# Three edits at the start of a fused state-attention and gated-projection kernel: a shorter first group of unread products, a constant first step on ACT, and the order of two loads

## The chip, the cores and the metric

The kernel runs on one core of a Trainium2 chip. The metric is device time in microseconds (us). The engines are TensorE (PE, with its weight loads shown as PEld), VectorE (DVE), ScalarE (ACT), GpSimd (POOL) and SyncE (SP), which issues the DMAs.

## What is computed

The reference has two stages. Cut to what matters:

```python
scores = (x @ state.T) / sqrt(D)                  # x: 8 x 8 x 512 x 64, state: 8 x 8 x 32 x 64
xread  = softmax(scores)  @ state                 # tokens read the state
sread  = softmax(scores.T) @ x                    # the state reads the tokens
x2     = concat([xread, sread], tokens)           # 8 x 576 x 512
gate   = sigmoid(sum(conv_w[k] * shift(x2, k)))   # causal convolution, 5 taps
out    = (gate * (x2 @ w_val)) @ w_out
```

All data is float32.

## The kernel before

The program is a list of numbered steps. `op(fn, ...)` appends one; the string `ORDER` says in which order they are issued, with a letter for the engine where a step may run on several (`a` ACT, `v` DVE, `g` POOL). Each engine works through its own instructions in that order, with semaphores between engines. So a number that moves in `ORDER` moves all that its step issues, on each engine it uses. Another table, `SLOTS`, gives every tile its buffer.

The eight batches follow each other, overlapped: scores on PE (`scores`, L386), maxima and 32x32 transposes on DVE (`max_n`, `probs`, L459, L469, L391), exponentials on ACT (L476, L396), subtraction of the maximum and the scaling on POOL (the helper at L238), reads of the state (L513 for batch 0, L498 for the others), values (L562), gates, and the output projection in three float32r terms (L571 to L573). Batch 0 is split in two runs of 256 tokens. The first run's data comes with the state in `first_in` (L263), the second run's in `rest_in` (L273), and both runs write the same two banks of PSUM, `sc`: DVE's transposes of the first run come before PE's second.

The convolution's taps come as 64-bit words, loaded by `load_conv` (L285, tile `cww`, 20 KB). ACT takes two parts of them (`words_part` L312, `words_side` L320, tiles `wt` and `ws`), DVE joins them (L328, L337, tile `cv`), and PE spreads them over partitions (L294, `cwbp`) for batch 0's reads. The weights `w_val` and `w_out` (tiles `vw` and `ow`) are joined in the same way; POOL does some of the parts (L322, `ws_v`).

`warm_up` (L347) issues products of a constant tile `blank` with itself, which nobody reads; `WARM` gives how many products each of four groups has. Step 955 is the first group and stands ahead of the first scores, 956 and 957 come after the second run, 958 ahead of the transposes `e2p` (L403). A product is two matmul records.

The steps at the start that the change and the prediction speak of: 66 `load_first`, 67 `load_xT` of batch 0 (`rest`), 6 `load_conv`, 69 and 70 `scores` of the two runs, 955 to 958 the unread products. Constants are set ahead of all steps: `blank` by DVE, `ident`, `edge`, `ex`, `sum2` and `own` by POOL. `own` (128x4) is a mask, 0 but for 1 in one column per group of 32 partitions; it is read only by `last_tokens`, far later.

A DMA uses one of eight semaphore lanes in turn, and a DMA that comes to a lane again waits for the landing of the one before it there.

Of the kernel before, what the change touches and what calls it, by code (L numbers as in the profile page):

```python
# [13 lines left out]
AF = mybir.ActivationFunctionType  # L14
# [24 lines left out]


STATES = 4
WARM = (8, 2, 5, 6)
TAP_COUNT = 5
ENGINES = dict(a="ACT", v="DVE", g="POOL")
ORDER = """
13 66 955 67 69 6 18 72 23 7 71 70 73 87 8a 89 9 74g 80 956 79 75 155 10 19 0 81 957 16 90 14 20g 76 82g 11 958 21 17a
77g 25a 38 24 15a 22 83 4 88 106g 53 94 92 1 26 84 157 85g 33 91 35g 27 95a 93a 28 100 78 12a 39 86 102a 158 101a 107
40a 30g 166 55a 54 262 167 41 168 56 159 57 160 29 42 169 34 111 113 115 112 116 31 2 119 264 36 32 37 114 120 117a
161g 273 265 43 58a 118g 59g 162 103 45a 68 44 104a 105a 121a 46 180 163 143 131 48 122g 64a 47 274 164g 137 123 149
# [69 lines left out]
def state_attention_gated_kernel(  # L119
# [17 lines left out]
    nc = tc.nc  # L137
    B, _, NJ, H, D = x_in.shape
    S, NPR, NS = NJ * P, sT_in.shape[3], sT_in.shape[4]
# [69 lines left out]
    def op(fn, *args):  # L209
        steps.append((fn, args))  # L210

    for name, shape, dt in (
# [6 lines left out]
    ident, wv, woh, wol, cv, cwt, edge, z, xt, ex, sum2, own, blank = (  # L219
        fixed[n,] for n in ("ident", "wv", "woh", "wol", "cv", "cwt", "edge", "z", "xt", "ex", "sum2", "own", "blank"))  # L220
# [441 lines left out]
    nc.gpsimd.memset(edge, -EDGE)  # L662
    nc.gpsimd.memset(ex[..., NS:], EPS)
    nc.gpsimd.memset(sum2, EPS)
    nc.gpsimd.memset(own, 0.0)
    for q in range(NPR):
        nc.gpsimd.memset(own[NS * q:NS * q + NS, q:q + 1], 1.0)

# [97 lines left out]
    def tail():  # L766
        for k in range(NPR):
            op(high, lambda k=k: weight_parts("wvh")[:, k], lambda k=k: wv[:, k])
            op(low, lambda k=k: weight_parts("wvl")[:, k], lambda k=k: wv[:, k], lambda k=k: weight_parts("wvh")[:, k])
        op(tail_high)  # L770
        op(tail_low)
        for m in range(2):
            for c in range(2):
                op(tail_first, m, c)
            for c in range(2):
                op(tail_taps, m, c)
            op(tail_gate, m)
            for c in range(2):
                op(tail_values, m, c)
            op(tail_gated, m)  # L780
            op(high, lambda m=m: get("tgh", m), lambda m=m: get("tg", m))
            op(low, lambda m=m: get("tgl", m), lambda m=m: get("tg", m), lambda m=m: get("tgh", m))
        for r in range(NR):
            for k in range(NPR):
                op(tail_project, r, k)
            op(tail_copy, r)
            op(tail_store, r)
# [25 lines left out]
    tail()  # L813
    for i, n in enumerate(WARM):
        op(warm_up, i, n)
# [55 lines left out]
```

## Time and profile before

| | |
|---|---|
| three runs | 205.43, 205.28, 204.87 us; median 205.28 |
| profiled execution | 205.45 us, of which the span of the trace is 203.6 |
| mean granted TensorE clock | 0.989 |
| PE busy | 194.9 us, 96% of the span |
| DVE busy | 171.4 us, 84% |
| POOL busy | 153.3 us, 75% |
| ACT busy | 144.4 us, 71% |
| DMA | 39.69 MB, 194 GB/s of HBM traffic over the span |

The profiled execution is 1.85 us longer than its span, the time from the first to the last instruction. Busy shares are means over the whole run; the stage that the change touches is the first 17 us of it.

### The profile page before, as it was taken

The numbers are of one execution on the slowest core, as the hardware profiler recorded it, in microseconds if no ns is written. First come the engines' busy times: TensorE is split into PE (matmuls) and PEld (weight loads), VectorE is DVE, ScalarE is ACT, GpSimd is POOL, SyncE is SP. The second block draws the span as 40 slices with busy tenths as digits, with TensorE's granted clock in tenths as the row PEclk, the third lists the DMA queues.
The fourth block names the chain that finished last, engine by engine and source line by source line (L and its number), as shares of the span: only waits on it lengthen the run. The fifth ranks groups of instructions, "written<-read, shape, count | busy, mean of one in ns | idle before, by whom it ended". The sixth has DMA issues, their size and how long they took to land.

```text
span 203.6 us, 4484 instructions
## 1 busy us (share of the span) xinstructions
PE 194.9 (96%) x1709; PEld 143.4 (70%) x1709; DVE 171.4 (84%) x278; ACT 144.4 (71%) x296; POOL 153.3 (75%) x119
## 2 busy tenths in 40 slices
PE   7599989799999999999999999999999999999993
PEld 7495344478567866687588557886876788899882
DVE  1898896999998999999999999999997995867002
ACT  0789996676988499878876989569947996612031
POOL 2594778797994889579997999599988998882200
PEclk9969999999999999999999999999999999999999
DMA  6999796059207928962982516250980380001736
GB/s 231 366 380 358 262 401 240 5 200 380 93 0 267 390 30 276 354 235 91 282 349 112 200 25 241 106 194 32 321 282 3 154 293 18 0 3 39 272 87 222
DMA packets 14787, 39.69 MB, mean 195 GB/s; under 512 B 1434, under 2 KB 5934, under 8 KB 12846
## 3 DMA queue, kind: packets, MB, share of 16 engines
q1 hardware_dynamic: 14766, 39.41, 54.3%
q8 instruction: 13, 0.21, 0.4%
q14 instruction: 8, 0.07, 0.1%
HBM read 26.30 MB, written 13.11 MB: 194 GB/s over the span
## 4 chain that ended last, share of the span: by engine, by line
PE 85%; DVE 9%; ACT 2%; issue 2%; DVEq 0%
PE val L562 22%; PE op L571 13%; PE op L572 13%; PE op L573 13%; PE xr L498 3%; PE warm L347 3%; PE tval L639 3%; PE sc L386 3%; PE xr L513 2%; PE sgv L357 2%; PE srp L427 2%; DVE g L567 2%; DVE sl L459 1%; DVE nb L391 1%; DVE acc L542 1%
## 5 line engine op out<-in xcount | busy, mean ns | idle before, releaser
L542 DVE SCALAR_TENSOR_TENSOR acc<-xr,cwt,acc 128x510 f32<-128x510 f32 (+2 forms) x84 | 59.1, 732 | 1.3 <-ACT xt L538 0.6
L571 PE MATMUL op<-woh,gh 128*128 128x512 f32 x124 | 50.3, 406 | 0.0
L572 PE MATMUL op<-wol,gh 128*128 128x512 f32 x124 | 48.4, 390 | 0.0
L573 PE MATMUL op<-woh,gl 128*128 128x512 f32 x124 | 48.3, 390 | 0.0
L238 POOL TENSOR_TENSOR gl<-g,gh 128x512 fp32r<-128x512 f32 x32 | 41.1, 1295 | 6.1 <-ACT gh L225 5.8
L238 POOL TENSOR_TENSOR acc<-acc,last 128x508 f32<-128x508 f32 x28 | 35.8, 1286 | 11.2 <-DVE acc L542 7.5
L571 PEld LDWEIGHTS op<-woh,gh 128*128 128x128 f32 x124 | 23.3, 188 | 11.6 <-issue 3.5
L573 PEld LDWEIGHTS op<-woh,gl 128*128 128x128 f32 x124 | 23.3, 188 | 5.0
L572 PEld LDWEIGHTS op<-wol,gh 128*128 128x128 f32 x124 | 23.3, 188 | 4.7 <-issue 0.5
L567 DVE SCALAR_TENSOR_TENSOR g<-sig,val 128x512 f32<-128x512 f32 x32 | 21.4, 675 | 5.0 <-PE val L562 2.1
L233 ACT ACTIVATE last<-xr,cwt 128x508 f32<-128x508 f32 x28 | 19.3, 698 | 5.3 <-DVE acc L542 3.7
L554 ACT ACTIVATE sig<-acc 128x512 f32<-128x512 f32 x28 | 17.9, 640 | 5.2 <-POOL acc L238 5.1
L225 ACT CAST gh<-g 128x512 fp32r<-128x512 f32 x29 | 18.1, 634 | 4.8 <-DVE g L567 4.8
L537 ACT ACTIVATE acc<-xr,cwt 128x512 f32<-128x512 f32 x28 | 19.2, 703 | 2.8 <-PE xr L498 2.8
L238 POOL TENSOR_TENSOR sl<-sl,mx 128x1024 f32<-128x1024 f32 (+1 forms) x9 | 15.6, 1729 | 6.9 <-DVE mx L469 6.9
L225 ACT COPY o<-op 128x512 f32<-128x512 f32 (+1 forms) x26 | 14.4, 570 | 7.0 <-PE op L573 5.1
L238 POOL TENSOR_TENSOR al<-sl,ah 128x1024 fp32r<-128x1024 f32 x7 | 16.8, 2397 | 1.1 <-ACT ah L225 1.1
L238 POOL TENSOR_TENSOR ex<-ex,rc 128x1024 f32<-128x1024 f32 (+1 forms) x9 | 15.5, 1723 | 2.5 <-DVE rc L481 2.3
L562 PE MATMUL val<-ah,swh 128*128 128x512 f32 x56 | 16.8, 396 | 0.5 <-DVE acc L542 0.3
L562 PE MATMUL val<-al,swh 128*128 128x512 f32 x56 | 16.8, 390 | 0.0
L562 PE MATMUL val<-ah,swl 128*128 128x512 f32 x56 | 16.4, 389 | 0.0
L227 DVE COPY o<-op 128x512 f32<-128x512 f32 x7 | 4.8, 690 | 13.7 <-PE op L573 13.7
(122 smaller groups left out, 375.4 us busy)
## 6 DMA issues: line engine op xcount, KB each, us to landing
x<-x_in SPq DMA_DIRECT2D x8, 1024.0 KB, 6.0
out<-o SPq DMA_DIRECT2D x31, 256.0 KB, 3.0
xT<-xT_in SPq DMA_DIRECT2D x7, 1024.0 KB, 6.6
turned<-eb SPq DMA_DIRECT2D x7, 512.0 KB, 3.0
e2T<-turned SPq DMA_DIRECT2D x7, 512.0 KB, 5.5
vw<-w_val SPq DMA_DIRECT2D x4, 511.8 KB, 6.8
ow<-w_out SPq DMA_DIRECT2D x4, 511.8 KB, 8.4
xT<-first_in SPq DMA_DIRECT2D x1, 576.0 KB, 3.4
```

The costliest lines, as they stand in the source:

```text
L225: nc.scalar.copy(out, in_)
L233: nc.scalar.mul(out, in_, factor)
L238: (nc.vector if e == "DVE" else nc.gpsimd).tensor_tensor(out, a, b, op=how)
L347: nc.tensor.matmul(get("warm", i)[:, j % 4 * P:j % 4 * P + P], blank, blank, start=True, stop=True)
L537: nc.scalar.mul(get("acc", b, pr), pt, cw[:, HALO, pr:pr + 1])
L542: nc.vector.scalar_tensor_tensor(acc[:, d:], get("xr", b, pr)[:, :S - d], cw[:, HALO - d, pr:pr + 1], acc[:, d:], op0=ALU.mult, op1=ALU.add)
L554: nc.scalar.activation(get("sig", b, pr), get("acc", b, pr), AF.Tanh, scale=0.5)
L562: nc.tensor.matmul(get("val", b, k), w[:, g, c], a[:, g], start=(term == 0 and g == 0), stop=(term == terms - 1 and g == NG - 1))
L567: nc.vector.scalar_tensor_tensor(get("g", b, k), get("sig", b, k), 1.0, get("val", b, k), op0=ALU.add, op1=ALU.mult)
L571: nc.tensor.matmul(pt, gh, woh[:, k], start=(k == 0), stop=False)
L572: nc.tensor.matmul(pt, gh, wol[:, k], start=False, stop=False)
L573: nc.tensor.matmul(pt, gl, woh[:, k], start=False, stop=(k == NPR - 1))
```

## The change

The first group of unread products has seven products and not eight. The load of the taps is issued ahead of the load of `rest`. The mask `own` is zeroed by an ACT instruction on the constant `blank`, relu(-1 x 1), in place of POOL's fill; it is ACT's first instruction, and the table load that precedes ACT's first activation comes with it. The rest of the order is kept.

```diff
-WARM = (8, 2, 5, 6)
+WARM = (7, 2, 5, 6)
...
 ORDER = """
-13 66 955 67 69 6 18 72 23 7 71 70 73 87 8a 89 9 74g 80 956 79 75 155 10 19 0 81 957 16 90 14 20g 76 82g 11 958 21 17a
+13 66 955 6 69 67 18 72 23 7 71 70 73 87 8a 89 9 74g 80 956 79 75 155 10 19 0 81 957 16 90 14 20g 76 82g 11 958 21 17a
...
-    nc.gpsimd.memset(own, 0.0)
+    nc.scalar.activation(own, blank[:, :NPR], AF.Relu, scale=-1.0)
     for q in range(NPR):
         nc.gpsimd.memset(own[NS * q:NS * q + NS, q:q + 1], 1.0)
```

SP's queue at the start of the program, before (left of the arrow is the tile written; `DMAHW1` is lane 1, and a wait on it here is for the landing of the DMA that had lane 1 last):

```order
L263 DMA xT_97<-first_in 128x1152
L273 DMA rest<-rest_in 128x1152
L285 DMA cww<-conv_w 20x511
L281 DMA vw_0_122<-w_val 128x2047
L269 DMA z<-z_in 128x512 [waits DMAHW0_49]
L281 DMA ow_3_212<-w_out 128x2047 [waits DMAHW1_49]
L281 DMA vw_3_239<-w_val 128x2047 [waits DMAHW2_49]
```

and now:

```order
L263 DMA xT_97<-first_in 128x1152
L285 DMA cww<-conv_w 20x511
L273 DMA rest<-rest_in 128x1152
L281 DMA vw_0_121<-w_val 128x2047
L269 DMA z<-z_in 128x512 [waits DMAHW0_49]
L281 DMA ow_3_211<-w_out 128x2047 [waits DMAHW1_49]
L281 DMA vw_3_238<-w_val 128x2047 [waits DMAHW2_49]
```

The taps and `rest` have changed places and lanes: lane 1 is now that of the taps, for which the `ow` behind `z` waits, and lane 2 that of `rest`.

ACT's queue from its first instruction on, before:

```order
L312 ACT_TABLE_LOAD [waits DMAHW2_49]
L312 ACTIVATE wt_conv<-cww,edge 20x128 [waits Pool_49]
L320 ACTIVATE ws_conv<-cww,edge 20x128
L476 ACTIVATE ex<-sl_124 128x2x8x32 [waits Pool_49]
L312 ACTIVATE wt_v_159<-vw_0_122,edge 128x512 [waits DMAHW3_49]
```

and now:

```order
L665 ACT_TABLE_LOAD
L665 ACTIVATE own<-blank 128x4 [waits DVE_49]
L312 ACTIVATE wt_conv<-cww,edge 20x128 [waits DMAHW1_49,Pool_49]
L320 ACTIVATE ws_conv<-cww,edge 20x128
L476 ACTIVATE ex<-sl_123 128x2x8x32 [waits Pool_49]
L312 ACTIVATE wt_v_158<-vw_0_121,edge 128x512 [waits DMAHW3_49]
```

The table load no longer waits for a DMA, and one activation stands behind it; the wait for the taps is now that of the first tap step.

POOL's queue behind its fills of `ex` and `sum`, as a difference:

```order
-L665 MEMSET own 128x4
 masks.py:199 ISA
 masks.py:199 AFFINE_SELECT ident<-ident 128x128 [waits Pool_49]
-L667 MEMSET own 32x1 [waits Pool_49] x2
+L667 MEMSET own 32x1 [waits Activation_49]
+L667 MEMSET own 32x1 [waits Pool_49]
 L667 MEMSET own 32x1 x2
```

The fills of ones stand where they did, and the first of them now waits for ACT.

## Rows read from the trace of the kernel before

**Rows 1.** The page, its part 4: the chain that ended last, by engine.

```profile
PE 85%; DVE 9%; ACT 2%; issue 2%; DVEq 0%
```

**Rows 2.** The chain that ended last, 0 to 45 us: start us, us, what.

```profile
1.04 3.79 PE warm L347 x16
...
5.53 0.79 DVE sl L459 x2
...
6.37 0.77 PE sc L386 x16
...
9.88 1.38 PE cwbp L294 x10
...
11.28 2.51 PE warm L347 x12
13.79 1.54 PE e2p L403 x8
...
16.79 5.08 PE xr L513 x80
```

**Rows 3.** Timeline, 0 to 16 us: start, duration, engine, line [idle before <- releaser].

```profile
0.73 0.38 SPq L263 DMA_DIRECT2D xT<-first_in  x1
...
1.17 0.42 SPq L273 DMA_DIRECT2D rest<-rest_in  x1
...
1.64 0.40 SPq L285 DMA_DIRECT2D cww<-conv_w  x1
...
4.76 0.66 PE L386 MATMUL sc<-xT 64*32 64x256 f32 x16
...
5.85 1.28 ACT L312 ACT_TABLE_LOAD   x1 [5.85 <-DMA cww<-conv_w]
6.10 0.33 SPq L281 DMA_DIRECT2D ow<-w_out  x1
...
6.37 0.67 PE L386 MATMUL sc<-rest,xT 64*32 64x256 f32 x16 [0.94 <-DVE sl L459]
...
6.96 1.83 PE L347 MATMUL warm<-blank 128*128 128x128 f32 x14
...
7.19 1.05 POOL L238 TENSOR_TENSOR sl<-sl,mx 128x512 f32<-128x512 f32 x1 [5.06 <-DVE mx L469]
```

**Rows 4.** DMA issues: what, KB each, median us from issue to landing.

```profile
xT<-first_in SPq DMA_DIRECT2D x1, 576.0 KB, 3.4
rest<-rest_in SPq DMA_DIRECT2D x1, 576.0 KB, 4.9
```

**Rows 5.** Line L386 to 16 us, PE's sequencer: ns min/median/max, first and last start.

```profile
L386 PEldq EVENT_SEMAPHORE  x2: 51/51/51, 6.1 to 13.7; - x2
```

**Rows 6.** By stretch: length, PE, PEld, DVE, ACT, POOL busy, granted clock, DMA share, GB/s.

```profile
3.50:4.00 0.50, 0.50 (x5) 0.50 (x4) 0.00 (x0) 0.00 (x0) 0.00 (x0) 1.00 1.01 406
...
5.50:6.00 0.50, 0.00 (x0) 0.00 (x0) 0.47 (x2) 0.15 (x1) 0.00 (x0) 1.00 0.26 107
```

**Rows 7.** The same for DVE alone: length, DVE busy, granted clock, DMA share, GB/s.

```profile
5.53:16.15 10.62, 10.28 (x24) 0.84 0.98 388
```

**Rows 8.** By stretch, all engines: columns as in rows 6.

```profile
11.60:15.02 3.42, 3.42 (x18) 3.42 (x18) 3.31 (x9) 2.80 (x7) 3.24 (x3) 0.50 1.02 384
```

**Rows 9.** Timeline, 11 to 16.2 us: third unread group, last exponential, last transpose.

```profile
11.21 2.58 PE L347 MATMUL warm<-blank 128*128 128x128 f32 x12
...
12.89 0.67 ACT L396 ACTIVATE e<-sc,nb 128x512 f32<-128x512 f32 x1
...
15.48 0.67 DVE L491 STREAM_TRANSPOSE a<-ex 128x512 f32<-128x512 f32 x1
```

**Rows 10.** Timeline, 19 to 25 us: POOL's part of w_val, and DVE's use.

```profile
19.91 1.96 POOL L322 TENSOR_SCALAR ws_v<-vw 128x512 f32<-128x512 int16 x1 [0.77 <-DMA vw<-w_val]
...
24.50 1.29 DVE L330 SCALAR_TENSOR_TENSOR wt_v<-wt_v,ws_v 128x512 int32<-128x512 f32 x2
```

**Rows 11.** Timeline at 41.67 us: a 128x4 copy on ACT.

```profile
41.67 0.15 ACT L538 COPY xt<-xr 128x4 f32<-128x4 f32 x1
```

## The prediction, made before the change was run

> **What bounds the kernel now.** First the chain that ended last: 85% of the span on it is TensorE (PE), 9% VectorE (DVE) [rows 1]. PE works through a fixed order almost without a hole, so only time taken out of this chain can shorten the run, and the change acts in the first microseconds alone. Then the same chain in order of time [rows 2]. It starts with the first group of unread products, 3.79 us from 1.04 on; between that group and DVE's two transposes stands the first run of score products; then come the second run at 6.37, later the spread taps at 9.88, another unread group, the transposes e2p at 13.79 and the reads xr at 16.79. ScalarE (ACT), GpSimd (POOL) and the DMAs do not stand on it here.
>
> Third, the timeline of the start [rows 3]. The first run of scores begins at 4.76, when the unread products have drained. Its data was there earlier: first_in was issued at 0.73 and landed 3.4 us later [rows 4], at 4.13. So the first group is too long by up to 0.63 us. The second run begins at 6.37, put down to DVE's transposes, which must leave the same two banks. Its data came shortly before: rest was issued at 1.17 and took 4.9 us [rows 4], so it landed at 6.07; SyncE (SP), which waits for the same landing to reuse its lane, issues ow at 6.10 [rows 3], and PE's sequencer passes its own wait on that DMA at 6.1 in 51 ns [rows 5]. So two conditions end within 0.3 us of each other ahead of the second run, and the change can move only the later one. That is what decides this case.
>
> **The change part by part.**
>
> *One unread product less.* The unread products of the third group, 12 records in 2.58 us [rows 9], run where the granted clock was 0.50 [rows 8], the 1.2 GHz level: 0.43 us for a product of two records. The first group takes 3.79 / 8 = 0.47 us a product with its fill and drain [rows 2], so it runs at that lower level too, though the column shows 1.00 ahead of its first recorded change; the second group, 14 records in 1.83 us [rows 3], runs at about half that. The saving on PE is 0.43 us: the first run of scores can start at 4.76 - 0.43 = 4.33, still 0.2 us after its data. That run may now start at the lower level. Between no slowing (0.66 us) and double (1.32 us) I take the middle, as half of it would lie ahead of 4.8, where it began before: +0.2 to +0.3. DVE's two transposes then end at 6.32 - 0.43 + 0.25 = 6.14, at best 5.89, at worst 6.55.
>
> *Taps ahead of rest.* SP issues cww at 1.17 and rest at 1.64, the slot that cww had [rows 3]: rest's issue is 0.47 us later. Whether its landing is, depends on what limits it. From 3.5 to 4.0, where first_in ends and rest begins, the DMA engines are fully busy and move 406 GB/s [rows 6]; rest was queued behind first_in, not short of an issue. Then it is late only by the 20 KB put ahead of it, 20 KB / 406 GB/s = 0.05 us. This is the value I take; the upper bound is the whole slot, 0.47 us, the lower one 0, since nothing brings rest forward. Rest lands at 6.07 + 0.05 = 6.12, PE's wait adds 0.05 and the start some 0.03: second run at 6.20 instead of 6.37. The transposes at 6.14 are just inside that. **Gain 0.17 us**; had rest not been late, up to 0.43; with both bounds the other way (transposes at 6.55 or rest at 6.54), a loss of 0.2 to 0.25.
>
> SP's later waits move with the lanes: ow (third from the front among those that wait) now waits for cww and not for rest, so it is issued by about 5.0 and not 6.10, and vw behind it waits for rest. The DMA engines are 98% busy from 5.53 to 16.15 [rows 7] and take what was issued in the same order, so I cost this at nothing.
>
> *ACT's first step on a constant.* Before, the table load begins at 5.85, released by cww, and takes 1.28 us [rows 3]; then come the two short tap steps and the first exponential, which needs POOL's subtraction, started at 7.19 by DVE's maximum and not by ACT. So the load is nearly hidden already, and taking it to the front gives 0 on the chain. It covers for the earlier start: DVE's maximum moves up by at most 0.43, and ACT would else have been late by about nothing. The step added is about 0.15 us, by a 128x4 copy on ACT [rows 11]. It makes POOL's four fills of own wait for table and step, to about 2.3 us, and queues nothing but them: POOL's next instruction starts at 7.19 [rows 3]. Cover: 4 us. The fills come after ident, so DVE's use of ident is not held up.
>
> **What carries through.** From 5.53 to 16.15 DVE is busy 10.28 of 10.62 us [rows 7]: it is behind on everything, so a shift of the second run (which its maxima wait for) moves cv, the taps, the exponentials and the last transpose of a, which ends at 16.15 [rows 9], by the same amount, and xr with it. Later, POOL's ws_v waits for a DMA that does not move, to 19.91 plus 1.96 = 21.87; DVE asks for it at 24.50 [rows 10], a slack of 2.6 us, so the gain isn't eaten there. The later loads are issued when compute frees their tiles and move along. Sum: 205.45 for the profiled execution, minus 0.17, is 205.28; that execution is 0.17 above the median, so against the median of 205.28 it is **205.1 us**.
>
> **Rivals.** A time within 0.3% (0.62 us) of 205.28, 204.66 to 205.9, cannot be told from no change by a measurement of this kernel.
>
> *The clock stays at the lower level* (the slower side). With a shorter first group and a longer hole behind the first scores, the level may come up a stretch later. The second group's 14 records would then take 0.215 - 0.131 us more each [rows 3, 9], 1.2 us, of which 1.1 fits in the hole ahead of 9.88; the ten tap records some 0.8 more (10 x 0.084); the third group runs at that level anyway. PE would come to e2p 0.9 us later, and as e2p leads straight to xr [rows 2], from the first tenth on it counts: 205.28 + 0.9 = 206.2. For it: the level fell once already, at 11.6 [rows 8], after holes like these. Against: PE is without a hole up to the end of the first scores in either version, only from 5.4 to 5.1. The Trainium skill, TensorE: Matmul & The Clock Gate (Why this matters for your kernels), asks for TensorE to be kept busy without holes from the start, and so speaks against a shorter group; the low pace of the first group agrees with its account that the clock starts throttled.
>
> *The fall at 11.6 doesn't happen.* Small shifts may as well avoid it. Then the third group is 12 x 0.084 = 1.0 us shorter and e2p waits for the exponential that ends at 13.56 instead [rows 9]; xr can then start when a is there, 16.15, and not at 16.72 to 16.79: 0.6 gained beside the 0.17, 204.5. Against it: PE's work ahead of the fall hardly changes.
>
> *The taps hold rest up by their whole slot or more.* Rest lands at 6.54 or a little later, PE starts at 6.62: 0.25 slower, 205.5. For it: the dip to 107 GB/s from 5.5 to 6.0 [rows 6] shows that the rings stall around small or new transfers. Against: full rings at the place where the taps now go. The Trainium skill, DMA: Bandwidth & Descriptors (Bandwidth, Measured), gives 0.68 us for 4 KB and 0.95 us for 64 KB; by that the estimate would be some 0.75 us for the taps if nothing overlapped, and 205.8.
>
> *The gain is taken back,* since another wait ends it later: 205.3. Against it stand the 2.6 us of slack above.
>
> **Numbers.** Forecast 0.50 (its own range 204.85 to 205.3); clock lower 0.12; clock better 0.15; taps hold rest up 0.15; gain taken back 0.08. Faster by over 0.3% is the better clock and 0.05 of the forecast's edge, as the runs shown lie 0.56 us apart: 0.20. Slower is the lower clock: 0.12. The rest, 0.68, is within 0.3%. The range from 204.5 to 205.8 takes in the taps' bounds and most of the better clock, and leaves out the lower clock and a third of the better one.
>
> **What would show it.** Right: first scores at about 4.3, second run at about 6.2 and now released by the DMA rest, not by DVE; ACT's table load ahead of 1 us and no wait on cww; xr at about 16.6. Wrong: rest landing past 6.3; the second unread group at 0.2 us a record; no granted 0.50 between 11 and 15 us; xr unmoved or later.

## The result, and the profile after

| | before | the change |
|---|---|---|
| runs, us | 204.87, 205.28, 205.35, 205.43 | 206.84, 209.75, 210.35, 210.47 |
| median, us | 205.31 | 210.05 |
| profiled execution, span, us | 205.45, 203.6 | 210.35, 208.5 |
| batch 0's second run of scores starts, us | 6.37 | 8.44 |
| xr of batch 0 starts, us | 16.79 | 21.66 |

The change is slower: the ratio is 1.0142, 95% interval 1.0098 to 1.0186. This ratio, like those below, leaves out executions over 1.5% above the fastest of the same kernel, here two of four, so the ratio of the medians, 210.05 / 205.31 = 1.023, is larger.

All of the difference arises ahead of xr. From the start of xr to the end of the span it is 203.6 - 16.79 = 186.8 us before and 208.5 - 21.66 = 186.8 us after. Of the 4.87 us by which xr starts later, 2.07 are there when the second run of scores starts, and 2.80 come between that run and xr.

The chain by engine, in the page of the change, against [rows 1]:

```profile
PE 84%; DVE 7%; DMA 3%; ACT 2%; issue 2%; SPq 0%; DVEq 0%
```

A DMA is now on the chain, 3% of it. The same chain in order of time (start us, us, what), against [rows 2]:

```profile
1.60 6.70 DMA rest<-rest_in
...
8.44 1.11 PE sc L386 x16
9.55 3.28 PE warm L347 x14
12.83 2.43 PE cwbp L294 x10
...
15.29 2.86 PE warm L347 x12
18.15 1.71 PE e2p L403 x8
...
21.66 5.11 PE xr L513 x80
```

The first unread group and DVE's transposes are gone from it: the load of `rest` has taken their place. Behind it, three rows of the same work are longer than before: scores 1.11 us (0.67 for the same 16 records in [rows 3]), second unread group 3.28 (1.83), spread taps 2.43 (1.38).

Landings, against [rows 4] (DMA issues: KB each, median us from issue to landing):

```profile
xT<-first_in SPq DMA_DIRECT2D x1, 576.0 KB, 3.4
rest<-rest_in SPq DMA_DIRECT2D x1, 576.0 KB, 6.7
```

`rest` was issued at 1.60 and landed at 8.30, not at 1.17 and 6.07. Its issue is 0.43 us later, its landing 2.23 us. The timeline of the start, against [rows 3]:

```profile
0.72 1.28 ACT L665 ACT_TABLE_LOAD   x1 [0.72 <-PEq L860]
...
2.02 0.20 ACT L665 ACTIVATE own<-blank 128x4 f32<-128x4 f32 x1
2.28 0.48 POOL L667 MEMSET own<- 32x1 f32 x4 [0.87 <-ACT own L665]
...
4.30 1.20 SPq L281 DMA_DIRECT2D ow<-w_out  x1
...
4.33 1.11 PE L386 MATMUL sc<-xT 64*32 64x256 f32 x16
4.35 0.37 ACT L312 ACTIVATE wt_conv<-cww,edge 20x128 f32<-20x128 int16 x1 [2.13 <-DMA cww<-conv_w]
...
5.54 0.78 DVE L459 STREAM_TRANSPOSE sl<-sc 128x256 f32<-128x256 f32 x2 [3.62 <-PE sc L386]
...
8.44 1.11 PE L386 MATMUL sc<-rest,xT 64*32 64x256 f32 x16 [3.00 <-DMA rest<-rest_in]
...
9.48 3.35 PE L347 MATMUL warm<-blank 128*128 128x128 f32 x14
...
9.68 1.96 POOL L322 TENSOR_SCALAR ws_v<-vw 128x512 f32<-128x512 int16 x1 [1.43 <-DMA vw<-w_val]
```

The early steps came as the edits ask: table load at 0.72, taps used at 4.35, first scores at 4.33. Then PE stands still for 3.00 us and is released by `rest`. The transposes had ended at 6.32, so the landing alone sets the second run. What the DMA engines did meanwhile (length, PE, PEld, DVE, ACT, POOL busy, granted clock, DMA share, GB/s), against [rows 6]:

```profile
3.00:3.50 0.50, 0.50 (x4) 0.50 (x4) 0.00 (x0) 0.00 (x0) 0.00 (x0) 1.00 1.05 364
3.50:4.00 0.50, 0.50 (x5) 0.50 (x3) 0.00 (x0) 0.00 (x0) 0.00 (x0) 1.00 0.65 83
4.00:4.50 0.50, 0.50 (x10) 0.28 (x17) 0.00 (x0) 0.15 (x1) 0.00 (x0) 1.00 0.45 101
4.50:5.00 0.50, 0.50 (x16) 0.05 (x8) 0.00 (x0) 0.50 (x2) 0.00 (x0) 1.00 1.01 157
5.00:5.50 0.50, 0.43 (x9) 0.00 (x0) 0.00 (x0) 0.06 (x1) 0.00 (x0) 1.00 0.59 163
5.50:6.00 0.50, 0.00 (x0) 0.00 (x0) 0.46 (x2) 0.00 (x0) 0.00 (x0) 1.00 0.53 220
6.00:6.50 0.50, 0.00 (x0) 0.00 (x0) 0.47 (x2) 0.00 (x0) 0.00 (x0) 1.00 0.78 299
```

Where 406 GB/s flowed before, 83 and 101 do. From 3.5 to 6.5 the six rates add up to 1023, so 1.26 us at 406 GB/s would have moved as much, and 1.74 us are lost. Before, a shorter dip stood around the taps where they were then (they landed at 5.85): 107 GB/s from 5.5 to 6.0 [rows 6], and as little in the half microsecond ahead of that:

```profile
5.00:5.50 0.50, 0.42 (x16) 0.00 (x0) 0.00 (x0) 0.00 (x0) 0.00 (x0) 1.00 1.03 124
```

`rest` landed just behind it, at 6.07, and `w_val` followed. Neither set the time: the second run waited for the transposes until 6.32, and `w_val` was first used at 8.32. Now a dip stands around the taps again, and `rest` is what follows them.

The granted clock reads 1.00 in all of these rows, but the pace of the products does not agree: 14 records in 3.35 us are the pace of the 1.2 GHz level, as in [rows 9], and not that of [rows 3]. The column reads 1.00 for the first group too, whose 14 records take 3.36 us, the same slow pace. So here the pace tells.

### The profile page after: what moved, and what is told of

Read it like the earlier page. It is cut to its first block, busy times and chain, and to the rows that moved or that the text cites. A ratio compares the mean times of both kernels' runs of the same rounds, so it can differ in the third digit from the quotient of the medians.

```text
span 208.5 us, 4480 instructions
## 1 busy us (share of the span) xinstructions
PE 198.8 (95%) x1707; PEld 145.9 (70%) x1707; DVE 171.6 (82%) x278; ACT 145.0 (70%) x297; POOL 153.2 (73%) x118
## 4 chain that ended last, share of the span: by engine, by line
PE 84%; DVE 7%; DMA 3%; ACT 2%; issue 2%; SPq 0%; DVEq 0%
PE val L562 21%; PE op L571 13%; PE op L572 12%; PE op L573 12%; DMA rest<-rest_in 3%; PE xr L498 3%; PE warm L347 3%; PE tval L639 3%; PE sc L386 3%; PE xr L513 2%; PE sgv L357 2%; PE srp L427 2%; DVE g L567 2%; PE cwbp L294 1%; DVE acc L542 1%
```

## The experiments

The theory has two parts. The late `rest` costs something in every execution; besides, in some executions TensorE stays at the lower level until about 20 us and that costs more. Rivals: the shorter group alone does it, or the new ACT step does, or one of these makes the clock stay down. All kernels below compute the whole reference. The first three diffs are against the kernel before, the others against the change; of `ORDER` only the head of its first line is shown. "Before" is the kernel before, run in the same job (medians 205.29 to 205.49).

### Each edit alone

**The shorter group alone.**

```diff
-WARM = (8, 2, 5, 6)
+WARM = (7, 2, 5, 6)
```

> The kernel before with the first group at seven products and nothing else. Theory A (the taps ahead of rest make rest land 2.2 us late, and the hole of 3 us on PE that this leaves keeps the clock at its lower level): here rest lands at about 6.1, the second run of scores starts at 6.1 to 6.4, the granted clock is at the upper level for the second unread group, 204.9 to 205.4 us. Rival B (the shorter group alone keeps the clock down): rest at 6.1, but the second unread group at 0.2 us a record, 206 to 208 us.

Measured: 205.08 us (204.49 to 205.30, 10 runs), ratio 0.9982 (0.9968 to 0.9997). Its timeline:

```profile
4.33 1.11 PE L386 MATMUL sc<-xT 64*32 64x256 f32 x16
...
6.38 1.11 PE L386 MATMUL sc<-rest,xT 64*32 64x256 f32 x16 [0.94 <-DVE sl L459]
```

The first run starts 0.43 us earlier and is 0.45 longer than in [rows 3], so the second starts where it did (6.37 before). It isn't this edit that costs; the small gain isn't in the start of this trace, where xr begins at 16.91.

**The taps' place alone,** with eight products and POOL's fill.

```diff
-13 66 955 67 69 6 18 72
+13 66 955 6 69 67 18 72
```

> The kernel before with the taps ahead of rest and nothing else; the first group has eight products. Theory A: rest lands at about 8.3 and not 6.1, the second run of scores starts at 8.4, the second unread group runs at the lower level, 208 to 210.5 us. Rival B: rest late as well, but the clock comes up as before, so that only the lateness of 2.1 us is paid, 207.4 us.

Measured: 206.83 us (five of 206.38 to 207.4 and one of 211.12), ratio 1.0068 (1.0045 to 1.0091). Five of the six lie at or below the 207.4 of the second forecast; the sixth is beyond the first. `rest` landed at 8.20. The chain, the timeline, and two stretches with the columns of [rows 6]:

```profile
1.60 6.60 DMA rest<-rest_in
```

```profile
8.34 0.67 PE L386 MATMUL sc<-rest,xT 64*32 64x256 f32 x16 [2.48 <-DMA rest<-rest_in]
...
12.01 1.66 PE L294 MATMUL cwbp<-cv,sel 20*128 20x128 f32 x10
```

```profile
9.22:12.62 3.40, 3.40 (x17) 3.17 (x17) 3.33 (x10) 1.61 (x4) 2.10 (x2) 0.50 1.00 396
12.63:20.00 7.37, 6.62 (x89) 4.75 (x96) 6.91 (x15) 7.01 (x16) 6.00 (x5) 1.00 0.86 325
```

This edit brings the late `rest`. The lower level lasts only to 12.62 in this execution (206.81 us), and xr starts at 18.51: 1.72 us later than before and not 4.87.

**ACT's step alone.**

```diff
-    nc.gpsimd.memset(own, 0.0)
+    nc.scalar.activation(own, blank[:, :NPR], AF.Relu, scale=-1.0)
```

> The kernel before with the mask zeroed by ACT and nothing else. Theories A and B: no change, 205.1 to 205.5 us, the table load at 0.7 us and hidden. A third possibility C (the early table load, which fetches tables while first_in and rest land, is what delays rest): rest at 7 us or later, 206 to 208 us.

Measured: 205.38 us (204.99 to 205.98, 10 runs), ratio 1.0002 (0.9987 to 1.0017). It costs and brings nothing that can be measured. Its timeline shows something else, with eight products and `rest` in time:

```profile
4.76 1.11 PE L386 MATMUL sc<-xT 64*32 64x256 f32 x16
...
6.81 0.67 PE L386 MATMUL sc<-rest,xT 64*32 64x256 f32 x16 [0.94 <-DVE sl L459]
```

The first run of scores takes 1.11 us here too, although it starts where it did before (4.76). So it isn't the shorter group that makes it long. And although the second run starts 0.44 us later than before, xr starts at 16.65, earlier than the 16.79 before.

**The change without the taps' move** (seven products, ACT's step).

```diff
-13 66 955 6 69 67 18 72
+13 66 955 67 69 6 18 72
```

> The changed kernel with the taps back behind rest: the group of seven and the mask on ACT stay. Theory A: rest at about 6.1, 204.9 to 205.4 us, all of the loss gone. Rival B: the loss of the clock stays, 206.5 us or more. C: the loss of the late rest stays, 207 us or more.

Measured: 205.42 us (204.95 to 205.58, 10 runs), ratio 0.9994 (0.9981 to 1.0008); second run at 6.38. With the taps back behind `rest` the whole loss is gone.

### The clock beside the late load

**The change with 14 products in the first group,** which shortens the standstill ahead of the second run.

```diff
-WARM = (7, 2, 5, 6)
+WARM = (14, 2, 5, 6)
```

> The changed kernel with fourteen products in the first group in place of seven, so that PE is busy to about 7 us and has a hole of some 0.5 us ahead of rest and not of 3 us. Theory A (late rest costs 1.5 us by itself; the rest of the loss, some 3.5 us, is the clock that stays down because of the hole): rest still lands at 8.3, but the upper level is there for the second unread group in every run, 206.4 to 207.2 us and none above 208. Rival (the clock has nothing to do with it, the late rest costs all): 209.5 to 210.5 us as with the change.

Measured: 207.19 us (206.41 to 207.82, 4 runs), ratio 1.0078 (1.0047 to 1.0109). Its timeline:

```profile
8.47 0.67 PE L386 MATMUL sc<-rest,xT 64*32 64x256 f32 x16 [1.59 <-DMA rest<-rest_in]
...
9.07 1.83 PE L347 MATMUL warm<-blank 128*128 128x128 f32 x14
...
11.98 1.38 PE L294 MATMUL cwbp<-cv,sel 20*128 20x128 f32 x10 [1.08 <-DVE cv L337]
```

The load is as late as in the change, these pieces have the upper level's length, and xr starts at 18.30. So the late load alone costs 1.5 us of start, and none of four executions lay near 210.

**The change with eight products,** to see whether the one product decides.

```diff
-WARM = (7, 2, 5, 6)
+WARM = (8, 2, 5, 6)
```

> The changed kernel with eight products in the first group, the one difference from it. Rest at about 8.3 as with the change. If the eighth product keeps the clock up more often: most runs at 206.4 to 207.4 us and at most one in four at 209.5 us or more, against half or more with seven. If the share has nothing to do with it: half of the runs at 209.5 us or more.

Measured: 206.42, 207.1, 207.18 and 209.15, 209.49, 210.48; ratio 1.0103 (1.0056 to 1.0149). Both groups of times are there. The profile is of the 209.15, columns as in [rows 6]:

```profile
8.05:9.15 1.10, 1.06 (x20) 0.68 (x21) 0.32 (x1) 0.45 (x1) 0.62 (x1) 1.00 1.05 428
9.16:19.40 10.24, 10.24 (x52) 8.94 (x58) 8.59 (x21) 6.63 (x16) 7.77 (x6) 0.50 0.88 349
```

PE was busy without a hole for 10.24 us at a granted 0.50, and xr starts at 20.49. The mean granted clock of the three shorter executions is 0.988 to 0.992, of the three longer ones 0.967 to 0.975: here the longer time goes with more time at the lower level. (In the change itself this mean doesn't tell: four of its six longer executions read 0.999 or 1.000.) The long time comes with eight products as well; whether the product taken away changes its share can't be told from so few executions.

**The change again,** for the spread of its times.

> The changed kernel once more, for how often the clock stays down. Theory A: two clusters, about 206.4 to 207.2 us and 209.5 to 210.5 us, with half of the runs or more in the upper one; the kernel with the taps ahead and eight products had 1 of 6 there. If the shorter group has no part in it, the share is one in six here too.

Measured: 206.4, 206.69, 206.71, 206.94 and 210.08, 210.34, 210.46; ratio 1.0065 (1.004 to 1.009). One more execution took 672.37 us, unlike all others; the profile fell on it, and nothing is read from it. With the first four runs that is five of eleven at 206.4 to 206.9 and six at 209.7 to 210.5.

### Which transfer stalls which

**The taps behind the first part of `w_val`.** Two ideas were in play: the dip follows the taps, or it belongs to the first reads of `w_val`.

```diff
-13 66 955 6 69 67 18 72
+13 66 955 67 69 18 6 72
```

> Seven products and the mask on ACT, with the taps behind the first part of w_val. Theory D (whatever the rings carry next after the taps stalls for 1 to 2 us, on all engines): rest lands at 5.4 to 5.6, before the stall, the dip in GB/s moves to 6 to 8 us and falls on the second part of w_val; vw_0 lands at about 7 us and not 8; time 205.0 to 205.6. Rival E (the stall belongs to the place, the first reads of w_val, and not to the taps): the dip stays at 5.0 to 6.0 us and rest lands at 5.5 to 6.1.

Measured: 205.44 us (204.58 to 206.18, 10 runs), ratio 0.9997 (0.9979 to 1.0015). `rest` landed at about 5.6, and no dip is left, neither behind the taps nor in `w_val`: the lowest half microsecond of 3.5 to 6 is this one (columns as in [rows 6]).

```profile
5.00:5.50 0.50, 0.43 (x10) 0.00 (x0) 0.00 (x0) 0.00 (x0) 0.00 (x0) 1.00 0.93 321
```

Both ideas fall in this form. The place in the queue matters, not the taps alone.

**The taps on ACT's queue.**

```diff
-        nc.sync.dma_start(get("cww")
+        nc.scalar.dma_start(get("cww")
```

> The changed kernel with the taps issued by ACT on its own queue, so that they are in other rings than rest. Theory D in the form that the ring behind the taps stalls: rest lands at 5.4 to 6.1 and the loss is gone, 204.9 to 205.4 us. If all transfers stall while the taps are served (a stall of the memory or the engines, not of the ring): a dip of the GB/s at 2 to 5 us, first_in or rest late by 1 us or more, 206 us or more.

Measured: seven of 205.16 to 206.35, then 207.94, 208.63 and 209.48; ratio 1.0011 (0.9981 to 1.0042). Most of the seven are near the first forecast, the three are not, and the profile is of one of the three, the 208.63. In it `rest` was issued at 1.16 and landed at 7.2, with 145 and 149 GB/s from 5.0 to 6.0. A dip remains, later and smaller, although the taps had left SP's queue. It isn't behind the taps at all: their first step runs at 2.95 without a wait for them, so they had landed two microseconds ahead of it.

```profile
2.95 0.37 ACT L312 ACTIVATE wt_conv<-cww,edge 20x128 f32<-20x128 int16 x1
```

So one dip, here, came with no short transfer next to it in SP's queue. What made it isn't shown, nor whether the seven shorter executions have it.

**Sixteen of the taps' twenty rows ahead of `rest`,** the other four behind it.

```diff
             nc.sync.dma_start(get("rest"), rest_in)
+            nc.sync.dma_start(get("cww").bitcast(I16)[16:NTP, :8 * NCV // 2 - 1], conv_w.bitcast(I16)[16:NTP, 1:])
...
-        nc.sync.dma_start(get("cww").bitcast(I16)[:NTP, :8 * NCV // 2 - 1], conv_w.bitcast(I16)[:, 1:])
+        nc.sync.dma_start(get("cww").bitcast(I16)[0:16, :8 * NCV // 2 - 1], conv_w.bitcast(I16)[0:16, 1:])
```

> The changed kernel with 16 of the 20 rows of the taps ahead of rest and the other 4 behind it. If the stall comes from the taps being spread over 10 of 16 DMA engines (uneven rings): no dip ahead of 5 us, rest at about 6.1, 205.0 to 205.5 us. If it comes from small rows of this tensor as such: rest late as with the change, 206.4 us or more.

Measured: six of 205.72 to 207.27 and four of 209.5 to 209.98, ratio 1.0039 (1.0016 to 1.0063). `rest` took 5.4 us and landed at 7.0: less late, not in time, and between the two forecasts. The dip is later and shallower, 249 and 222 GB/s from 5.0 to 6.0.

**1 MB of `w_val` ahead of `rest`,** taps behind it: `rest` late, but for its bytes.

```diff
-13 66 955 6 69 67 18 72 23 7
+13 66 955 69 18 23 67 6 72 7
```

> Seven products and the mask on ACT, the taps behind rest, but two parts of w_val (1 MB) ahead of rest, so that rest is late by bytes alone: at some 400 GB/s it lands at about 8 us. Theory A (lateness is what costs, whatever makes it): second run of scores at about 8.1, and two clusters, 206 to 207 us and 209 to 210.5 us, as with the change. Rival (the stalled transfers behind the taps do the harm elsewhere, by late weights): 205.0 to 205.8 us, for the weights are early here.

Measured: 208.19 us (207.65 to 208.44, 4 runs), ratio 1.014 (1.011 to 1.0169). `rest` landed at 9.03, a microsecond later than forecast, and there is one group of times, not two; neither forecast is met.

**The states of step 0 (192 KB) ahead of `rest`,** taps behind it: a short transfer in wide rows.

```diff
-13 66 955 6 69 67 18 72 23 7
+13 66 955 0 67 69 6 18 72 23 7
...
-10 19 0 81
+10 19 81
```

> Seven products and the mask on ACT, the taps behind rest, and the load of the states (192 KB, 128 rows of 1.5 KB on all 16 DMA engines) in the place ahead of rest. If any transfer put there makes the rings stall: rest at 7 us or later, 206.4 us or more. If the taps' small rows do it: rest late by its bytes alone, 192 KB at 400 GB/s or 0.5 us, so at 5.9 to 6.5; 205.0 to 205.7 us.

Measured: 206.41 and three of 208.91 to 209.14, ratio 1.0144 (1.0096 to 1.0192). The same stretch, first with `w_val` ahead, then with the states (columns as in [rows 6]):

```profile
3.50:4.00 0.50, 0.50 (x5) 0.50 (x3) 0.00 (x0) 0.00 (x0) 0.00 (x0) 1.00 1.02 412
4.00:4.50 0.50, 0.40 (x2) 0.10 (x1) 0.00 (x0) 0.00 (x0) 0.00 (x0) 1.00 1.04 409
```

```profile
3.50:4.00 0.50, 0.50 (x5) 0.50 (x3) 0.00 (x0) 0.00 (x0) 0.00 (x0) 1.00 1.01 261
4.00:4.50 0.50, 0.50 (x10) 0.26 (x17) 0.00 (x0) 0.00 (x0) 0.00 (x0) 1.00 1.16 194
```

A long transfer in that place leaves the rate alone, and of the 2.96 us by which `rest` is late the 1 MB takes 2.6 at 406 GB/s. The states, 192 KB, bring the dip back, and `rest` lands at 7.80: 1.73 us late, of which their own bytes take 0.48 at that rate. So it doesn't take the taps' narrow rows. The first kernel also tells something of the clock: its PE stood still for 3.56 us ahead of the second run, longer than in the change, but none of its four executions shows the longer time.

**The taps ahead of all loads.**

```diff
-13 66 955 6 69 67 18 72
+13 6 66 955 67 69 18 72
```

> Seven products and the mask on ACT, with the taps ahead of first_in, the first transfer of all. If what follows the taps on the rings stalls: first_in lands at 5 us or later and not at 4.1, the first scores start there, 206.4 us or more. If only the boundary to rest is sensitive: first_in at 4.6 (its issue is 0.45 later), rest at 5.5 to 6.1, 205.2 to 205.7 us.

Measured: nine of 205.22 to 205.91 and one of 209.21, ratio 1.0005 (0.999 to 1.002). No dip between 3.5 and 6.0 (341 to 424 GB/s); `first_in` landed at 4.9, `rest` at 6.3, both a little later than forecast. The lowest rate of that stretch:

```profile
3.50:4.00 0.50, 0.50 (x5) 0.50 (x3) 0.00 (x0) 0.00 (x0) 0.00 (x0) 1.00 0.96 341
```

A short transfer in front of everything leaves no dip behind it. This also settles another rival: `rest` was issued at 1.59, as late as in the change (1.60), so its later issue is not what makes it late there. But the profile is of the 209.21, and xr starts at 20.53 in it with the pace of the lower level, although `rest` came in time (PE had waited 0.53 us for `first_in`).

**Taps, then `w_val`, then `rest`.** If what follows a short transfer in that place stalls, whatever it is, it must now be `w_val`.

```diff
-13 66 955 6 69 67 18 72
+13 66 955 69 6 18 67 72
```

> Seven products and the mask on ACT; the queue is first_in, taps, first part of w_val, rest. Theory F (a short transfer right behind first_in leaves the next one, whichever it is, not ready, and the rings run dry): a dip of the GB/s from 3.5 to 5.5 us, now on w_val, which lands at 7 us or later; rest behind it at 8.5 to 9.5; 207 us or more. Theory G (only reads of rest stall when they don't follow first_in directly): no dip ahead of 5 us, w_val lands at 5.6 to 6.0, rest, late by bytes, at 7 to 8.

Measured: 207.89, 208.16, 208.54, 210.31; ratio 1.016 (1.012 to 1.02). The timeline, then the rate behind the taps (columns as in [rows 6]):

```profile
7.84 1.96 POOL L322 TENSOR_SCALAR ws_v<-vw 128x512 f32<-128x512 int16 x1 [0.19 <-DMA vw<-w_val]
...
9.33 1.11 PE L386 MATMUL sc<-rest,xT 64*32 64x256 f32 x16 [4.49 <-DMA rest<-rest_in]
```

```profile
4.00:4.50 0.50, 0.50 (x18) 0.22 (x17) 0.00 (x0) 0.14 (x1) 0.00 (x0) 1.00 0.72 221
...
5.00:5.50 0.50, 0.00 (x0) 0.00 (x0) 0.50 (x2) 0.07 (x1) 0.00 (x0) 1.00 0.37 102
```

`w_val`, in the place that `rest` has in the change, lands at about 7.8, and `rest` behind it at 9.19. That `rest` itself has something about it falls. What stands right behind the short transfer behind `first_in` comes late, and all behind it in the queue with it.

## Why the prediction was wrong, point by point

**The step that failed** is in *Taps ahead of rest*: "Then it is late only by the 20 KB put ahead of it, 20 KB / 406 GB/s = 0.05 us. This is the value I take; the upper bound is the whole slot, 0.47 us". Measured: 2.2 us. Full rings at 3.5 to 4.0 [rows 6] were taken as a property of the place; they were a property of which transfer followed which. The row that warned was read and was in the argument: 107 GB/s right behind the taps in the kernel before [rows 6]. It was set beside the rival and not taken as a hole that moves onto `rest`. It was also read too short, as the dip begins at 5.0, with 124 GB/s. Even so it would have been too small: the two rows lose 0.5 x (2 - 231 / 406) = 0.72 us, the dip of the change 1.74. The estimate of 0.75 us, worked out from the Trainium skill, DMA: Bandwidth & Descriptors (Bandwidth, Measured), was too small as well; the table there is of loads issued from GpSimd over 128 partitions, and the taps are issued from SP over 20.

**The rival that named the place had the wrong size, and two rivals were one.** "The taps hold the rest up" gave 205.5 and "the clock stays at the lower level" 206.2, with chances of their own. The late load alone costs 1.4 to 1.7 us (206.83 with the taps' move alone, xr 1.51 to 1.72 later in the two profiles above), and with it, in six of eleven executions of the change, came the stay at the lower level. In the four kernels whose `rest` landed in time behind `first_in` (the shorter group, ACT's step, both, and the taps behind `w_val`) none of 40 executions lay above 206.2, and none of the 82 of the kernel before in the same jobs above 206.51.

**The clock's price** was put at 0.9 us; the executions of the change are 3.5 us apart (means 206.72 and 210.24). The prediction let the second group's slower records fall into the hole ahead of the spread taps and counted 0.8 for the taps. In the change's profile, between the second run and xr, scores are longer by 0.44, the second group by 1.52, the taps by 1.12, the third group and e2p by 0.35 and 0.17, and batch 1's scores with what stands behind them, up to xr, by 0.35 (1.80 and 1.45). Less the hole of 1.09 us ahead of the taps, now filled, that is 2.9; 2.80 is what the start of xr shows. Where the level rises at 12.62 instead (the taps' move alone, 206.81 us), the third group takes 1.60 us and not 2.58, and second run to xr is 10.17 us, 0.25 below the 10.42 before. With `rest` 0.1 earlier as well, xr starts 2.80 + 0.25 + 0.10 = 3.15 us ahead of that in the change's profile; the other 0.4 or so of the 3.5 lies behind xr.

**The first scores** start at 4.33, as forecast, but take 1.11 us, +0.45 and not the +0.25 taken, inside the bounds. So the transposes end at 6.32, as in the profile of the kernel before. The base was at fault, more than the cut: 0.66 us is one execution's length. In the three other profiles with eight products (ACT's step alone, the taps' move alone, the change with eight) the first run takes 1.11 us from 4.75 or 4.76 on, and the transposes end at about 6.75. Against these the cut of a product does bring the second run forward where `rest` comes in time, from 6.81 to 6.38; with the taps moved it brings nothing, for `rest` sets that run.

**ACT's first step** was right in each part: load at 0.72, step 0.20 us (0.15 taken), fills ended at 2.76, ratio 1.0002 by itself. Beside it, the `ow` behind `z` was forecast for about 5.0 and issued at 6.25, since the two issues ahead of it on SP took 1.20 and 0.65 us (0.47 and 0.54 before).

**What carries through** was right behind xr: from there to the end it is between 186.4 and 187.0 us in the profiles used here. Ahead of xr it was wrong that a shift of the second run moves xr by as much. With ACT's step alone and with the change without the taps' move that run starts at 6.81 and 6.38, and xr at 16.65 and 16.67, as the second unread group takes 1.83 us in the one and 2.84 in the other; in the change 2.07 us became 4.87. So even the 0.17 need not have come out at the end, and "the gain isn't eaten" spoke of a gain that was not there. POOL's `ws_v` also slid, from 8.33 in the kernel with the shorter group to 9.68. `w_val` stands behind `rest` in SP's queue and came later with it, so that is no second cause. The Trainium skill, DMA: Bandwidth & Descriptors (Queues, rings and completion order), says that each DMA engine takes up descriptors in the order of its ring, which agrees.

**What stays open.** Why a transfer behind a short one stalls there, but not behind a long one, nor behind a short one at the very front, isn't shown; nor is the dip with the taps on ACT's queue, which has no short transfer beside it. With the taps right behind `first_in` and `rest` behind them, four profiles show `rest` landing at 7.95 to 8.34 (the change, the taps' move alone, 8 and 14 products); most other orders of the queue have one profile each. What decides whether the clock stays down isn't either: a late load goes with it, yet 14 products gave 0 of 4 executions, the longer standstills of 3.56 us (behind 1 MB of `w_val`) and 4.49 us (behind the taps and 512 KB) 0 and 1 of 4, and one of ten came with the load in time. Nor is the gain of 0.0018 with the shorter group alone explained; with ACT's step beside it, the gain can't be told from nothing.

## What to carry to other kernels

Price a moved load by what stands behind it in the queue, and measure it with that edit alone: 20 KB put ahead of 576 KB made it 2.2 us late, some forty times what the bytes take. A dip in the DMA rate that hurts nobody now can be a cost for whoever is moved there. Take a row as the base of a sum only if more than one execution shows it: with eight products the first scores took 0.66 us in one profile and 1.11 in three. And when a load feeds TensorE's first work, a late landing may cost twice, once for the wait and once for the level at which the engine then runs.

## What the runs showed of the hardware that was not expected

- **A short transfer right behind the first large one leaves the next one late.** 20 KB or 192 KB there: 83 to 261 GB/s from 3.5 to 4.5 us in the profiles of the change and of the states' kernel (284 and 304 with 14 products, where `rest` is as late), and what follows comes 1.7 to 2.3 us late (`rest` at 7.80 to 8.34, not 6.07; `w_val` at about 7.8). 1 MB there: 409 to 412 GB/s. The taps first of all, or behind 512 KB of `w_val`: no dip. One dip, with the taps on ACT's queue, had no short transfer beside it.
- **One program, two times.** Eleven executions of the change (without the one of 672.37) fall into 206.4 to 206.9 and 209.7 to 210.5, with nothing between. The Trainium skill, TensorE: Matmul & The Clock Gate (What's actually happening), says that the slow start varies from run to run, which agrees, and puts it below 1% of a typical span; here the two times are 3.5 / 206.7 = 1.7% apart.
- **The clock column can hide this.** It reads 1.00 in the change's profile up to 20 us, mean 0.999 over the span, though the spread taps take 2.50 us and not 1.38. The length of a repeated instruction is the safer sign.
